# Experts with 640 slots, results scattered straight to the output, weights cast in the load

## The chip, the core and the metric

The kernel runs on one core of a Trainium2 chip. The core has five engines with a queue of instructions each: TensorE (PE, matrix multiplication; PEld is its loading of weights), VectorE (DVE), ScalarE (ACT), GpSimd (POOL) and SyncE (SP). Sixteen DMA engines move data between DRAM and the on-chip memory SBUF; a transfer is issued by an instruction on the queue of SP, ACT or POOL. The engines run apart from one another and wait on semaphores. PSUM is the memory that matmuls write to. The metric is device time in microseconds (us) of one execution.

## The reference

Attention with a bias by relative distance, then a layer of eight experts that each token is sent to by a hash of its id. There are 8 batches, 8 heads, 576 positions and 64 values a head, so 4608 tokens of 512 values; an expert has a hidden layer of 1024.

```python
scores = scale * q @ k.T + bias_table[bucket(|i - j|)]     # 8 x 8 heads, 576 x 576
attn   = softmax(scores);  x = attn @ v                     # 4608 rows of 512
e      = token_ids * 2654435761 % 8                         # one expert a token
out[i] = relu(x[i] @ w1[e[i]]) @ w2[e[i]]                   # w1 512x1024, w2 1024x512
```

The multiplier is 1 modulo 8, so the expert is the low three bits of the token id. The inputs are a fixed draw, with 584, 594, 556, 565, 570, 567, 568 and 604 tokens for experts 0 to 7.

## The kernel before

The program is written with a library that tracks which instruction reads or writes which tile or DRAM tensor, adds the waits, and orders each engine's queue with a planner of its own: it goes by the order of the program, but lets an instruction that is ready rise past others that are not. The order in a queue is therefore not that of the text. In the trace the zero fill written after batch 0 (L357) is issued at 19.84 us, and the load of the first expert's w1, written in batch 4 (L373), at 96.10 us.

**Set-up (L89 to L183).** The exponential of the bias goes over a small DRAM tensor t_ebp. From the token ids the kernel works out, for each token, its slot: 768 (CAP) times its expert plus its rank among that expert's tokens. The ids are read so that the token's position is on the partitions, one 4-byte word at a time. The ranks come from a one-hot tile by a doubling sum on DVE and a triangular matmul. The slots are ds2.

**Attention (L186 to L364).** For each batch v is loaded on SP's queue, and q and k on POOL's, which turns them from 32 to 16 bits on the way. Four head pairs follow. For each pair PE transposes q and k (L251), forms scores (L289), ACT takes the exponential (L297), DVE multiplies by the bias tile (L305), PE multiplies with v (L330), and DVE divides into x_sb (L348). The bias tiles are made in batch 0, per head, by two transfers on SP's queue (L195, t_ebr from t_ebp, and L203, the tile from t_ebr). Finished 128-row groups of x_sb are scattered by POOL into the DRAM tensor t_xperm at their slots (L364), 36 groups in all. t_xperm was filled with zeros before (L357), by SP.

**Experts (L379 to L457).** For expert e the kernel loads w1 and w2 in 32 bits on SP's queue (L414, L422), casts them on ACT (L419) and on DVE (L427), loads the expert's 768 rows (xpn, L388), transposes them on PE (L399, copied by DVE at L404), multiplies by w1 (L434; 2 halves of 384 columns, 8 blocks of the hidden layer, 4 steps each), takes ReLU on ACT (L440) and multiplies by w2 (L448; 6 groups of 128 rows, 8 steps each). DVE copies each group to a tile ok (L455, four buffers), and SP writes it to the DRAM tensor t_pout (L457). The transposes of the next expert stand between the two layers. The first expert's w1 is loaded and cast during attention (L373, L377).

**Tail (L458 to L468).** For each of 36 groups of tokens, POOL gathers the rows from t_pout at the same slots (L460), into one of twelve tiles, and SP writes the tile to the output (L468).

Of the kernel before, what the change touches and what calls it, by code (L numbers as in the profile page):

```python
# [11 lines left out]
F32 = mybir.dt.float32  # L12
F16 = mybir.dt.float16
I32 = mybir.dt.int32
AF = mybir.ActivationFunctionType
# [16 lines left out]
def kernel(  # L32
# [23 lines left out]
    CAP = 768  # L56
    NSLOT = E * CAP
    NPT = DM // P
# [13 lines left out]
    SLT_np = np.triu(np.ones((P, P), dtype=np.float32), 1)  # L72
    Z_np = np.zeros((P, DM), dtype=np.float16)
# [4 lines left out]
    Z_d = nc.inline_tensor(Z_np, "t5_zero")  # L78
# [4 lines left out]
    xperm_d = nc.dram_tensor("t5_xperm", [NSLOT, DM], F16, kind="Internal")  # L83
    pout_d = nc.dram_tensor("t5_pout", [NSLOT, DM], F32, kind="Internal")

# [5 lines left out]
    w1f0 = cst.tile([P, NPT, F], F32, name="w1f0")  # L91
    w1h0 = cst.tile([P, NPT, F], F16, name="w1h0")

    with tc.tile_pool(name="su", bufs=1, side="right") as su, tc.tile_pool(
# [18 lines left out]
        sltsb = su.tile([P, P], F32, name="sltsb")  # L113
        nc.sync.dma_start(out=sltsb[:, :], in_=SLT_d.ap())

        tid32 = moe_token_ids.bitcast(I32)
        e2i = su.tile([P, NGT], I32, name="e2i")
        with nc.allow_non_contiguous_dma("tiny index reshape"):
            nc.sync.dma_start(
                out=e2i[:, :],  # L120
                in_=bass.AP(tid32.tensor, 0, [[2, P], [2 * P, NGT]]),
            )
        ei = su.tile([P, NGT], I32, name="ei")
        nc.vector.tensor_scalar(
            out=ei[:, :], in0=e2i[:, :], scalar1=E - 1, scalar2=None,
            op0=ALU.bitwise_and,
        )
        ef = su.tile([P, NGT], F32, name="ef")
        nc.vector.tensor_copy(out=ef[:, :], in_=ei[:, :])

        oh = su.tile([P, E, NGT], F32, name="oh")
        for e in range(E):
# [4 lines left out]
        rowtot = su.tile([P, E], F32, name="rowtot")  # L137
        nc.vector.tensor_reduce(
            out=rowtot[:, :], in_=oh[:, :, :], axis=mybir.AxisListType.X,
            op=ALU.add,  # L140
        )
        partA = sup.tile([P, E], F32, name="partA", space=bass.MemoryType.PSUM)
        nc.tensor.matmul(out=partA[:, :], lhsT=sltsb[:, :], rhs=rowtot[:, :])

        pa = su.tile([P, E, NGT], F32, name="pa")
        pb = su.tile([P, E, NGT], F32, name="pb")
        nc.vector.tensor_copy(out=pa[:, :, :], in_=oh[:, :, :])
        cur, nxt = pa, pb
        sh = 1
        while sh < NGT:  # L150
            nc.vector.tensor_copy(out=nxt[:, :, :sh], in_=cur[:, :, :sh])
            nc.vector.tensor_tensor(
                out=nxt[:, :, sh:], in0=cur[:, :, sh:],
                in1=cur[:, :, : NGT - sh], op=ALU.add,
            )
            cur, nxt = nxt, cur
            sh *= 2
        exc = nxt
        nc.vector.tensor_tensor(
            out=exc[:, :, :], in0=cur[:, :, :], in1=oh[:, :, :], op=ALU.subtract  # L160
        )
        for e in range(E):
            nc.vector.tensor_scalar(  # L163
                out=exc[:, e, :], in0=exc[:, e, :],
                scalar1=partA[:, e : e + 1], scalar2=None, op0=ALU.add,
            )
        nc.vector.tensor_tensor(
            out=exc[:, :, :], in0=exc[:, :, :], in1=oh[:, :, :], op=ALU.mult
        )
        rank = su.tile([P, NGT], F32, name="rank")  # L170
        nc.vector.tensor_reduce(
            out=rank[:, :], in_=exc[:, :, :].transpose([0, 2, 1]),
            axis=mybir.AxisListType.X, op=ALU.add,
        )
        dsf = su.tile([P, NGT], F32, name="dsf")
        nc.vector.tensor_scalar(
            out=dsf[:, :], in0=ef[:, :], scalar1=float(CAP), scalar2=None,
            op0=ALU.mult,
        )
        nc.vector.tensor_tensor(  # L180
# [318 lines left out]
```

The softmax here doesn't subtract the row's maximum and nothing guards it: scores larger than these inputs give would overflow.

## Time and profile before

| | |
|---|---|
| median of 3 runs | 699.89 us (699.37 to 702.21) |
| span of the profiled execution (the page gives no other time of it) | 705.6 us |
| set-up and wait for the first bias tile | 0 to 57.4 us |
| attention | 57.4 to 440.5 us |
| last scatters and first load of rows | 440.5 to 463.6 us |
| experts | 463.6 to 643.6 us |
| tail | 643.6 to 705.6 us |
| busy: PE, DVE, ACT, POOL | 556.6, 343.5, 290.3, 139.7 us |
| DMA queues: hardware_dynamic (SP), software_dynamic (POOL) | 86.28 MB, 23.60 MB |

The page cuts the span in 40 slices of 17.6 us and gives each engine's busy share of a slice as a digit of tenths. Groups of instructions carry their line, engine, what they write and read, count, busy time and mean; after the second bar stands the idle time of the engine before them and what ended it. The chain is followed back from the last instruction to what released it, and its parts are given as start, duration and what. A timeline's line has start, duration, engine, line and instruction, and in brackets the idle time before it with its releaser. In a table of stretches the DMA share is the sum of the time of packets over 16 engines, so it can pass 1 where packets overlap. Bytes are those written: the q and k loads count at 16 bits.

### The profile page before, as it was taken

To read this page: it belongs to the slowest core of one execution; us is meant where nothing else is said; L and a number is where in the kernel's file an instruction comes from. 1 tells how busy PE (TensorE), PEld (TensorE's weight loads), DVE (VectorE), ACT (ScalarE), POOL (GpSimd) and SP (SyncE) were. 2 spreads that over 40 slices of the span, in tenths; PEclk is the share of its full clock that TensorE was granted. 3 is DMA by queue.
4 is the path that set the end of the run, shared out by engine and by line. 5 is a ranking of instruction groups with operands and counts; after the bars stand their busy time and mean duration, and the time that the engine had idled before them with its cause. 6 is when DMAs were issued, how large, how long until landed. Compare 5 with 4: busy or idle time off the path is not lost.

```text
span 705.6 us, 9655 instructions
## 1 busy us (share of the span) xinstructions
PE 556.6 (79%) x3656; PEld 287.1 (41%) x3656; DVE 343.5 (49%) x1150; ACT 290.3 (41%) x458; POOL 139.7 (20%) x156
## 2 busy tenths in 40 slices
PE   2626999999999999999999998089999999994000
PEld 0202545444444545454444544055555555552000
DVE  3305666666676766667666666024433343312000
ACT  1312365545545453645445463044466545440000
POOL 7213001412323124114110200200000000002772
PEclk9999999999999999999999999999999999998555
DMA  9999980900905819409300000197999997113998
GB/s 111 307 206 262 274 220 24 134 25 18 132 31 33 103 39 67 84 16 86 72 15 1 31 1 1 53 380 278 322 370 334 326 359 265 45 76 127 359 392 283
DMA packets 159614, 110.49 MB, mean 157 GB/s; under 512 B 120520, under 2 KB 131912, under 8 KB 159472
## 3 DMA queue, kind: packets, MB, share of 16 engines
q1 hardware_dynamic: 79952, 86.28, 39.0%
q0 software_dynamic: 79616, 23.60, 26.9%
q8 instruction: 28, 0.46, 0.3%
q14 instruction: 18, 0.15, 0.1%
HBM read 92.55 MB, written 35.54 MB: 182 GB/s over the span
## 4 chain that ended last, share of the span: by engine, by line
PE 64%; DMA 10%; ACT 9%; issue 5%; DVE 3%; POOL 3%; SPq 3%; POOLq 0%; ACTq 0%
PE px L330 22%; PE sc L289 15%; PE ops L448 11%; PE hps L434 11%; ACT attn L297 8%; DMA t_ebr<-t_ebp 3%; POOL og L460 3%; DVE attn L305 3%; PE psq L251 3%; SPq L218 2%; PE psk L251 2%; DMA t_xperm<-x_sb,ds 2%; DMA ebias<-t_ebr 1%; DMA w1f<-in_moe_w_dram 1%; PE xps L399 1%
## 5 line engine op out<-in xcount | busy, mean ns | idle before, releaser
L297 ACT ACTIVATE attn<-sc 128x576 f16<-128x576 f32 (+1 forms) x320 | 197.4, 647 | 224.6 <-PE sc L289 198.4
L330 PE MATMUL px<-vaug,attn 128*128 128x65 f16 (+3 forms) x1600 | 182.4, 243 | 20.0 <-DVE attn L305 16.8
L289 PE MATMUL sc<-qT,kT 64*128 64x512 f16 (+3 forms) x640 | 178.0, 428 | 24.6 <-ACT attn L297 24.4
L305 DVE TENSOR_TENSOR attn<-attn,ebias 128x576 f16<-128x576 f16 (+1 forms) x320 | 139.3, 452 | 90.5 <-ACT attn L297 57.6
L330 PEld LDWEIGHTS <-attn 128*128 128x128 f16 (+3 forms) x1600 | 117.4, 122 | 126.5 <-DVE attn L305 77.4
L440 ACT ACTIVATE h<-hps 128x384 f16<-128x384 f32 x128 | 62.2, 490 | 98.3 <-PE hps L434 97.5
L434 PE MATMUL hps<-xpt,w1h 128*128 128x384 f16 x512 | 86.6, 330 | 1.5 <-ACT h L440 1.5
L448 PE MATMUL ops<-w2h,h 128*128 128x512 f16 x384 | 86.6, 379 | 0.0
L364 POOL DMA_INDIRECT t_xperm<-x_sb,ds x36 | 37.6, 1044 | 243.6 <-DVE x_sb L348 178.2
L289 PEld LDWEIGHTS <-kT 64*128 64x128 f16 (+1 forms) x640 | 46.4, 116 | 79.6 <-issue 71.5
L460 POOL DMA_INDIRECT og<-t_pout,ds x36 | 34.1, 947 | 205.3 <-DMA t_pout<-ok 193.2
L348 DVE TENSOR_SCALAR x_sb<-px,rcp 128x64 f16<-128x64 f32 (+1 forms) x320 | 70.0, 274 | 1.6
L434 PEld LDWEIGHTS <-w1h 128*128 128x128 f16 x512 | 50.6, 99 | 36.3 <-issue 3.5
L455 DVE COPY ok<-ops 128x512 f32<-128x512 f32 x48 | 33.1, 691 | 59.5 <-PE ops L448 53.3
L448 PEld LDWEIGHTS <-h 128*128 128x128 f16 x384 | 37.1, 98 | 41.2
L224 POOL DMA_DIRECT2D qb<-in_q_dram x40 | 35.4, 886 | 82.7 <-PE psk L251 73.8
L404 DVE COPY xpt<-xps 128x768 f16<-128x768 f16 x32 | 17.2, 556 | 62.5 <-PE xps L399 61.6
L343 DVE RECIPROCAL rcp<-px 64x1 f32<-64x1 f32 (+1 forms) x128 | 18.7, 167 | 51.9 <-PE px L330 48.9
L251 PE MATMUL psq<-ident,qb 128*128 128x128 f16 (+1 forms) x160 | 35.6, 292 | 9.0 <-DVE pb L163 5.1
L228 POOL DMA_DIRECT2D kb<-in_k_dram x40 | 35.3, 882 | 21.9 <-DMA kb<-in_k_dram 21.8
L251 PE MATMUL psk<-ident,kb 128*128 128x128 f16 (+1 forms) x160 | 36.3, 297 | 0.0
L399 PE MATMUL xps<-ident,xpn 128*128 128x128 f16 x192 | 15.9, 230 | 22.1 <-DMA xpn<-t_xperm 22.1
(37 smaller groups left out, 182.5 us busy)
## 6 DMA issues: line engine op xcount, KB each, us to landing
w1f<-in_moe_w_dram SPq DMA_DIRECT2D x8, 2048.0 KB
w2f<-in_moe_w_dram SPq DMA_DIRECT2D x8, 2048.0 KB
t_pout<-ok SPq DMA_DIRECT2D x48, 256.0 KB
out_dram<-og SPq DMA_DIRECT2D x36, 256.0 KB
vb<-in_v_dram SPq DMA_DIRECT2D x32, 256.0 KB
xpn<-t_xperm SPq DMA_DIRECT2D x8, 768.0 KB
ebias<-t_ebr SPq DMA_DIRECT2D x8, 720.0 KB
qb<-in_q_dram POOLq DMA_DIRECT2D x32, 128.0 KB
```

What stands on the lines that cost most here:

```text
L224: nc.gpsimd.dma_start(out=qb16[:nt, t, :, :], in_=q[b, :, P * t : P * t + nt, :].transpose([1, 0, 2]),)
L251: nc.tensor.transpose(out=pst[:, P * t : P * t + nt], in_=srct[:nt, t, 2 * m : 2 * m + 2, :], identity=ident[:nt, :nt],)
L289: nc.tensor.matmul(out=scps[hh][:nt, ns:ne], lhsT=kT[64 * hh : 64 * hh + 64, P * t : P * t + nt], rhs=qT[64 * hh : 64 * hh + 64, ns:ne], s ...
L297: nc.scalar.activation(out=attn[hh][:nt, t, :], in_=scps[hh][:nt, :], func=AF.Exp, bias=0.0, scale=scale,)
L305: nc.vector.tensor_tensor(out=attn[hh][:nt, t, :], in0=attn[hh][:nt, t, :], in1=ebias[2 * m + hh][:nt, NJT - 1 - t, :], op=ALU.mult,)
L330: nc.tensor.matmul(out=px[nbase : nbase + isz, c, :], lhsT=attn[hh][:nt, t, i0c : i0c + isz], rhs=vaug[hh][:nt, t, :], start=(imm == 0), s ...
L348: nc.vector.tensor_scalar(out=x_sb[nbase : nbase + isz, gt, h * D : (h + 1) * D], in0=px[nbase : nbase + isz, c, :D], scalar1=rcp[nbase : ...
L364: nc.gpsimd.indirect_dma_start(out=xperm_d.ap()[:, :], out_offset=bass.IndirectOffsetOnAxis(ap=ds2[:, g : g + 1], axis=0), in_=x_sb[:, g, ...
L434: nc.tensor.matmul(out=hps[:, :], lhsT=w1h[:, kt, ts(ft, P)], rhs=xpt[kt][:, ts(nr, NR)], start=(kt == 0), stop=(kt == NPT - 1),)
L440: nc.scalar.activation(out=h1[:, ft, ds(nr * NR, NR)], in_=hps[:, :], func=AF.Relu, bias=0.0, scale=1.0,)
L448: nc.tensor.matmul(out=ops[:, :], lhsT=h1[:, ft, ts(kc, P)], rhs=w2h[:, ft, :], start=(ft == 0), stop=(ft == NFT - 1),)
L460: nc.gpsimd.indirect_dma_start(out=og[:, :], out_offset=None, in_=pout_d.ap()[:, :], in_offset=bass.IndirectOffsetOnAxis(ap=ds2[:, g : g + ...
```

## The change

Each expert gets 640 slots instead of 768. Tokens beyond 640 of an expert go to extra rows of t_xperm, one for each token, and are worked by a separate path at the end, inside a branch on a flag that the set-up computes (some expert has more than 640 tokens). A row of t_xperm is 514 instead of 512 values: the last two hold the token's number as a 32-bit integer, and rows without a token hold a number out of range. After the second layer POOL scatters each 128 rows straight to the output, at the numbers that came along with the rows; rows out of range are left out. t_pout and the tail are gone.

The weights are loaded on POOL's queue and turned to 16 bits by the transfer, into two tiles each for w1 and w2 that last the whole kernel; those of experts 0 and 1 are written in batches 3 and 5 of attention, those of e+2 after the layer of e that frees the tile. Loads of rows are written two experts ahead, three buffers. In the first layer one activation covers both halves (320 columns each). The set-up reads the ids in rows of 128 and transposes them on PE, takes the ranks from two matmuls and a scan, and the fill of t_xperm is issued from ACT's queue, from an SBUF tile.

```diff
-    CAP = 768
+    CAP = 640
     NSLOT = E * CAP
+    NROW = NSLOT + B * S
+    BIG = 1 << 20
...
+    XW = DM + 2
+    xperm_d = nc.dram_tensor("t5_xperm", [NROW, XW], F16, kind="Internal")
...
+    w1t = [cst.tile([P, NPT, F], F16, name=f"w1t{i}") for i in range(2)]
+    w2t = [cst.tile([P, NFT, DM], F16, name=f"w2t{i}") for i in range(2)]
+    def load_w1(e):
+        nc.gpsimd.dma_start(
+            out=w1t[e % 2][:, :, :],
+            in_=moe_w1[e].rearrange("(kt p) f -> p kt f", p=P),
+        )
+    def load_w2(e):
+        nc.gpsimd.dma_start(
+            out=w2t[e % 2][:, :, :],
+            in_=moe_w2[e].rearrange("(ft p) d -> p ft d", p=P),
+        )
...
-                in_=bass.AP(tid32.tensor, 0, [[2, P], [2 * P, NGT]]),
+        er = su.tile([NGT, 2 * P], I32, name="er")
+        nc.sync.dma_start(
+            out=er[:, :],
+            in_=bass.AP(tid32.tensor, 0, [[2 * P, NGT], [1, 2 * P]]),
+        )
...
+        zx = su.tile([P, XW], F16, name="zx")
+        nc.vector.memset(zx[:, :DM], 0.0)
+        nc.vector.memset(zx[:, DM:XW].bitcast(I32), BIG)
+        nc.scalar.dma_start(
+            out=xperm_d.ap()[:NSLOT, :].rearrange("(p r) d -> p r d", p=P),
+            in_=zx[:, :].unsqueeze(1).to_broadcast([P, NSLOT // P, XW]),
+        )
...
-            if b == 0:
-                nc.sync.dma_start(
-                    out=xperm_d.ap().rearrange("(a b) d -> a (b d)", b=64),
...
-            if b == 4:
-                nc.sync.dma_start(
-                    out=w1f0[:, :, :],
-                    in_=moe_w1[0].rearrange("(kt p) f -> p kt f", p=P),
-                )
-                nc.scalar.copy(out=w1h0[:, :, :], in_=w1f0[:, :, :])
+            if b == 3:
+                load_w1(0)
+                load_w2(0)
+            if b == 5:
+                load_w1(1)
+                load_w2(1)
...
+            xpn = mo.tile([P, NSC, XW], F16, name="xpn", bufs=3)
...
+        xn = {0: x_load(0), 1: x_load(1)}
+        xt = {0: x_transpose(xn[0])}
         for e in range(E):
...
+            if e + 2 < E:
+                xn[e + 2] = x_load(e + 2)
+            w1h, w2h = w1t[e % 2], w2t[e % 2]
...
+            for ft in range(NFT):
+                hps = mop.tile([P, NRC, 512], F32, name="hps", bufs=2,
+                               space=bass.MemoryType.PSUM)
+                for nr in range(NRC):
...
+                nc.scalar.activation(
+                    out=h1[:, ft, :].rearrange("p (r n) -> p r n", r=NRC),
+                    in_=hps[:, :, :NR], func=AF.Relu, bias=0.0, scale=1.0,
+                )
+            if e + 2 < E:
+                load_w1(e + 2)
+            if e + 1 < E:
+                xt[e + 1] = x_transpose(xn[e + 1])
+            for kc in range(NSC):
+                ops = mop.tile([P, DM], F32, name="ops", bufs=2,
+                               space=bass.MemoryType.PSUM)
...
                 ok = mo.tile([P, DM], F32, name="ok", bufs=4)
                 nc.vector.tensor_copy(out=ok[:, :], in_=ops[:, :])
-                nc.sync.dma_start(out=pout_d.ap()[ts(kg, P), :], in_=ok[:, :])
-        for g in range(NGT):
...
+                nc.gpsimd.indirect_dma_start(
+                    out=out[:, :],
+                    out_offset=bass.IndirectOffsetOnAxis(
+                        ap=xn[e][:, kc, DM:XW].bitcast(I32), axis=0
+                    ),
+                    in_=ok[:, :],
+                    in_offset=None,
+                    bounds_check=N - 1,
+                    oob_is_err=False,
+                )
+            if e + 2 < E:
+                load_w2(e + 2)
+
+    over = nc.values_load(flag[:1, :1], min_val=0, max_val=1)
+    with tc.If(over > 0):
...
```

What is left out after the branch is the path for tokens beyond 640: for each expert it loads both weights again and runs a loop of 36 turns, each with a gather, both layers for 128 rows and a scatter.

## The prediction

> **What bounds the kernel now.** I read the page's slices first, then the stretches with the engines' busy times, the chain that ended last, and the engines' own timelines. The four stretches that matter, with the columns us, then busy time (instructions) of PE, PEld, DVE, ACT, POOL, then PE clock, DMA share, GB/s:
>
> ```profile
> PE   2626999999999999999999998089999999994000
> DMA  9999980900905819409300000197999997113998
> ...
> 440.40:463.60 23.20, 2.05 (x19) 1.92 (x20) 1.79 (x6) 0.00 (x0) 4.80 (x5) 1.00 0.36 115
> 463.60:705.60 242.00, 178.47 (x1072) 98.11 (x1070) 66.77 (x86) 87.00 (x135) 34.08 (x36) 0.88 0.77 278
> 643.60:705.60 62.00, 0.00 (x1) 0.00 (x0) 0.69 (x1) 0.00 (x0) 34.08 (x36) 0.54 0.87 312
> ```
>
> Attention occupies 57 to 440 us with PE full; a gap follows; the experts run to 643.6; then PE is idle for 62.0 us while rows are gathered and written. So everything after the first expert matmul is 242.0 us, and this is where the change acts. In the expert stage PE has no pauses worth naming: one expert, from its first matmul to the next one's, is 578.56 - 556.41 = 22.15 us.
>
> ```profile
> 556.41 10.40 PE hps L434 x64
> 566.81 0.67 PE xps L399 x12
> ...
> 568.84 9.71 PE ops L448 x45
> 578.56 10.40 PE hps L434 x64
> ```
>
> The gap and the start are DMA. Five scatters stand one behind another at the end of attention; each waits for the one before to have landed (same columns as the timeline: start, us, engine, line, then in brackets the idle time and what ended it):
>
> ```profile
> 443.62 0.96 POOL L364 DMA_INDIRECT t_xperm<-x_sb,ds  x1 [2.20 <-DMA t_xperm<-x_sb,ds]
> 446.78 0.96 POOL L364 DMA_INDIRECT t_xperm<-x_sb,ds  x1 [2.19 <-DMA t_xperm<-x_sb,ds]
> ...
> 648.52 0.97 POOL L460 DMA_INDIRECT og<-t_pout,ds  x1 [0.30 <-issue]
> 649.79 0.94 POOL L460 DMA_INDIRECT og<-t_pout,ds  x1 [0.30 <-issue]
> ```
>
> The reader should see the two paces: scatters into one DRAM tensor come every 3.15 us, gathers into separate tiles every 1.25 us. The difference is a wait of a write for the write before it, not the cost of an indirect transfer.
>
> In the start, this stretch of the chain leads to the first multiplication with the bias at 57 to 60 us (start, us, what):
>
> ```profile
> 18.73 6.73 DMA t_ebp<-ebsb
> 26.01 23.56 DMA t_ebr<-t_ebp
> 49.63 10.16 DMA ebias<-t_ebr
> ```
>
> 0.9 MB of t_ebr takes 23.56 us because the 6.3 MB zero fill was issued at 19.84 us on the same SP queue, just ahead.
>
> **The change, part by part.**
>
> *Slots, 768 to 640.* Of 22.15 us, 64 matmuls of the first layer take 10.40 (384 columns, 162.5 ns each); at 320 columns 135.4 ns, so 8.67. The second layer has 40 matmuls instead of 48: 10.36 to 8.63. Transposes 20 instead of 24: 1.39 to 1.16. PE's time of an expert becomes 18.45 us. ReLU on 640 columns: the 576-column activation takes 647 ns and the 384-column one 490, so about 0.70 us against the 1.08 us in which PE fills it; hidden.
>
> *Weights cast in the DMA.* ACT's cast (3.60 us) and DVE's (2.28) go; both lie beside PE in the expert stage. The one of w1h0 at 118.28 us isn't hidden: that head pair took 132.68 - 118.11 = 14.57 instead of 12.2 us; I take -2.4. The loads move to POOL's queue, which the page calls software_dynamic, and of which there is one. How long is a 2 MB load there? Before shows no such load, so I bound it. From below: the uncast loads of the same size move 393 GB/s in 466 to 474 us, 5.3 us. From above: the q and k loads are cast, in runs of 256 B, and their 128 KB (after the cast) come every 0.87 us, which is 301 GB/s of fp32; POOL's issue sets that pace, so a 2 MB load needs at most 7.0 us unless long runs are slower than short ones. I take T = 6.
>
> *Scatter of the results.* Removed: 48 writes to t_pout and the tail's 36 gathers and 36 output writes, 62.0 us on the path. Added: 40 scatters on POOL, all into the one tensor out. By the rows at 443 us I expect each to wait for the one before: s = 3.15 us with 1 KB rows is the low end; these rows have 2 KB, so the part that is neither issue nor pause (3.15 - 0.96 - 0.71 = 1.5 us) at most doubles: 4.6 is the high end. The bytes alone at 393 GB/s add 0.33, so I take s = 3.5.
>
> Now what is queued behind what. POOL's order in the stage is w1(e+2), five scatters, w2(e+2), w1(e+3), five scatters. One queue drains in order (t_ebr behind the fill is the row for that), so the first scatter of an expert lands only after two loads have. Let t0 be the first expert matmul. First layer done at 8.7; w1(2) issued (0.9), 0.4 to start; scatter 0 lands at 11.6 + T (1.6 for its own landing); the fifth starts 0.7 + 3s later, at T + 12.3 + 3s = 28.8. From the fifth scatter of one expert to that of the next: two issues and a start 2.0, two loads 2T, landing 1.9, pause 0.7, 3s: 2T + 4.6 + 3s; the first issue overlaps by 0.3, so 2T + 4.3 + 3s = 26.8 us. That is longer than PE's 18.45: POOL's queue becomes the bound. Five such intervals; one with one load (T + 4.3 + 3s); one with none (5s); the last landing (s). Sum: 12T + 38.1 + 27s = 72 + 38.1 + 94.5 = 204.6 us. The ends are 187 (5.3; 3.15) and 246 (7.0; 4.6).
>
> PE isn't a second bound in that loop: with four ok tiles it runs a whole expert ahead of the scatters, so the load of w1(e+3) finds its buffer free when POOL comes to it. Were it not so, up to 8.7 us an expert would be added.
>
> A rule speaks against this part. POOL's issue of a scatter takes 0.96 us at the end of attention, where DVE is idle, and up to 1.30 in the middle. The Trainium skill (SBUF — State Buffer, "Who interferes with whom") says that copies in DVE's two-port modes shut GpSimd out of a shared port, and advises issuing from ACT or SP. If it held here at the 1.30 end, 27 x 0.34 = 9 us would be added; DVE's copies in this stage read PSUM, so I leave the sum.
>
> *Overflow path.* The drawn token ids give 556 to 604 tokens an expert, all below 640, so the branch isn't taken. The flag's load and the jump over the branch have no row; the chain's last piece, 1.16 us on POOL's sequencer, is the nearest. Bounds 0 and 10 (five engines with a few such pieces); I take 5, nearer to neither, since every engine has to read the flag.
>
> So from the first expert matmul: 209.6 against 242.0, -32.4.
>
> *Gap.* xpn shrinks from 768 to 640 rows of 1028 B instead of 1 KB: 4.79 to about 4.3; -0.5. Five scatters stand as before.
>
> *Start.* Three things move. The token ids came as 4608 runs of 4 B ahead of the v loads on SP, landing at 11.7 us; now 36 rows. The fill goes to ACT's queue, 5.26 MB, early, so t_ebr no longer stands behind it: at the 10.16 us of the three times larger ebias load it could take 15 us less. Against it: the scheduler lets independent loads rise (w1f0, written in batch 4, was issued at 96.1 us; the fill, written after batch 0, at 19.84), and POOL stands idle from 24.8 to 36.7, so the four weight loads, 8.4 MB instead of 2.1, may fall into this stretch: at 393 GB/s 16 us more DMA beside the bias loads. The fill also occupies ACT's queue ahead of the exponential that feeds t_ebp. Bounds -15 and +12; I take -5. The Trainium skill (DMA: Bandwidth & Descriptors, "Queues, rings and completion order") has each engine take turns between queues, packet by packet; by that the bias loads would get half of the rate, and -5 would be about 0.
>
> The set-up's DVE operations are each under 0.7 us and end before 26 us, beside the wait for bias; nothing.
>
> Sum: -32.4 - 2.4 - 0.5 - 5 = -40.3. The profiled execution has a span of 705.6 us (the page gives no other time for it), 5.7 over the median of the runs, 699.9; I carry the difference: 665.3 by the span, 660 by the median.
>
> **The rivals.**
>
> *PE stays the bound.* If scatters into out don't wait for one another, or the loads don't hold them up, eight experts take 8 x 18.45 = 148, plus last copy, scatter and branch, some 9: 157 against 242, with the rest -93: 607; with a pace of five scatters plus two issues (19.3 us) 615. For it: the gathers' 1.25 us. Against: all 36 scatters before have the wait.
>
> *The cast loads are slow (slower than before).* Each us of T costs 12. With 2.4, 0.5 and 5 gained elsewhere the balance turns where 12T + 137.6 = 250, T = 9.4 us, 224 GB/s. At T = 12 the time is 732. For it: no long cast in the trace; against: 301 GB/s on much shorter runs.
>
> *The start gets dearer.* If weights and fill delay the bias loads by 12 instead of helping by 5, 677. For it: DMA digits of 9 through the first 88 us.
>
> **How the numbers follow.** Forecast (POOL's queue the bound) 0.62, 660; its own range 630 to 695 from the ends of T, s and the start taken one at a time. PE the bound 0.14, 611. Dear start 0.10, 677. Slow casts 0.14, above 700. The range 606 to 704 leaves out the slow case and a sliver. About 0.5% (3.5 us) is what a measurement can tell from no change. Faster: 0.60 + 0.14 + 0.09 = 0.83; within: 0.04; slower: 0.13.
>
> **What would show it.** In the profile after: POOL the releaser, with scatter waits on "DMA out"; a period of some 27 us from expert to expert; PE's idle time in the stage ended by weight or ok waits; first-layer matmuls of 320 columns near 135 ns; no gather tail; the first bias multiplication before 57 us. I am wrong if scatters come under 2 us apart (then 611), if w1 or w2 takes over 9 us to land, or if the first scatter of x, at 99.0 us before, starts later.

## The result and the profile after

The changed kernel takes 722.05 us (median of 5 runs, 720.98 to 726.58) where the kernel before takes 699.89 (median of 5, 698.62 to 702.21): 1.0325 times as long, interval 1.0293 to 1.0357. It is slower, and the time lies above the range of the prediction (606 to 704). The profiled executions differ by 724.7 - 705.6 = 19.1 us.

The slices of the changed kernel, and its table of stretches cut at the same events as before (first bias multiplication, last scatters of x, first expert matmul, end; columns as in the prediction):

```profile
PE   2016069999999999999999999834997769569670
DMA  9999997409149093091391000003477656766511
...
0.00:94.60 94.60, 19.03 (x76) 6.33 (x76) 10.54 (x49) 9.81 (x14) 26.62 (x35) 1.00 1.37 177
94.60:477.60 383.00, 357.08 (x2493) 180.68 (x2493) 262.47 (x1004) 190.21 (x308) 76.90 (x84) 1.00 0.47 65
477.60:501.40 23.80, 1.68 (x15) 1.54 (x16) 1.57 (x6) 0.00 (x0) 4.79 (x5) 1.00 0.33 105
501.40:724.70 223.30, 160.31 (x980) 92.27 (x977) 41.76 (x71) 45.05 (x64) 49.89 (x52) 0.86 0.54 115
```

Read against the table of before, the four stretches were 57.4, 383.0, 23.2 and 242.0 us. The tail is gone (no slices of PE 0 at the end), and the experts with all behind them take 18.7 us less. Attention and the gap stand still within 1 us. The start takes 37 us more. That is the whole result: -18.7 in the stage that was forecast to give -32.4, +37 where -5 was forecast.

**The start.** SP's queue in the changed kernel, from its timeline (start, duration, queue, line, instruction), then DVE's first bias multiplication:

```profile
3.65 57.90 SPq L267 DMA_DIRECT2D vb<-in_v_dram  x10
61.68 3.68 SPq L130 DMA_DIRECT2D t_ebp<-ebsb  x1
76.61 1.84 SPq L244 DMA_DIRECT2D t_ebr<-t_ebp  x3
83.25 4.55 SPq L252 DMA_DIRECT2D ebias<-t_ebr  x3
```

```profile
94.56 1.92 DVE L354 TENSOR_TENSOR attn<-attn,ebias 128x576 f16<-128x576 f16 x5 [27.29 <-DMA ebias<-t_ebr]
```

The same in the kernel before:

```profile
3.07 15.55 SPq L218 DMA_DIRECT2D vb<-in_v_dram  x5
18.73 1.06 SPq L111 DMA_DIRECT2D t_ebp<-ebsb  x1
19.84 0.56 SPq L357 DMA_DIRECT2D t_xperm<-t_zero  x1
...
57.44 1.93 DVE L305 TENSOR_TENSOR attn<-attn,ebias 128x576 f16<-128x576 f16 x5 [23.50 <-DMA ebias<-t_ebr]
```

From the table t_ebp all bias tiles are made. Ahead of it now stand ten loads of v instead of five, and they take 57.9 us in all instead of 15.6. It goes out 43 us later (61.68 against 18.73). From there to the first multiplication it is 32.9 us instead of 38.7, so the gain that the prediction saw behind t_ebp is there, 5.8 us, and is dwarfed by what happened ahead of it. The lines of DMA queues and issues on the changed kernel's page show what the v loads ran beside, and the waits of SP's queue what they waited for (who, for what, us in total, times, longest):

```profile
q10 hardware_dynamic: 5136, 5.26, 4.3%
...
t_xperm<-zx ACTq DMA_DIRECT2D x1, 5140.0 KB, 47.8
...
SPq L267 <- DMA t_xperm<-zx: 23.2, 1, 23.2
```

The fill, now on a queue of its own, went out at 1.64 us and landed 47.8 us later, in 5136 packets of about 1 KB. Four loads of v went out by 26.3 us; the fifth waited 23.2 us, until the fill had landed at 49.4, and the last six took from 49.45 to 61.56. The wait is the program's, not one for data: in the trace the transfers of SP and ACT take eight semaphores in turn (108 to 115) to signal that they have landed, and each first waits for the transfer that had its semaphore before; the fill had 111, and so has the fifth load.

**The experts.** POOL's timeline over one expert of the changed kernel; in brackets the idle time before each instruction and what ended it:

```profile
565.20 0.98 POOL L489 DMA_INDIRECT out_dram<-ok,xpn  x1 [7.64 <-DMA out_dram<-ok,xpn]
566.33 0.81 POOL L102 DMA_DIRECT2D w1t<-in_moe_w_dram  x1 [0.16 <-issue]
568.58 1.00 POOL L489 DMA_INDIRECT out_dram<-ok,xpn  x1 [1.45 <-DMA out_dram<-ok,xpn]
577.49 0.97 POOL L489 DMA_INDIRECT out_dram<-ok,xpn  x1 [7.91 <-DMA out_dram<-ok,xpn]
581.91 0.97 POOL L489 DMA_INDIRECT out_dram<-ok,xpn  x1 [3.45 <-DMA out_dram<-ok,xpn]
582.88 0.97 POOL L108 DMA_DIRECT2D w2t<-in_moe_w_dram  x1
585.41 1.00 POOL L489 DMA_INDIRECT out_dram<-ok,xpn  x1 [1.56 <-issue]
593.57 0.99 POOL L489 DMA_INDIRECT out_dram<-ok,xpn  x1 [7.16 <-DMA out_dram<-ok,xpn]
```

Each scatter waits for the one before to land. Quiet ones follow every 3.5 us (581.91 to 585.41); one that is under way beside a weight load holds the next back for 8 to 9 us (568.58 to 577.49, 585.41 to 593.57). Five gaps, two of them long, make 28.4 us an expert. The page's groups tell who pays:

```profile
L488 DVE COPY ok<-ops 128x512 f32<-128x512 f32 x40 | 27.7, 691 | 138.2 <-DMA out_dram<-ok,xpn 121.0
L489 POOL DMA_INDIRECT out_dram<-ok,xpn x40 | 39.2, 981 | 155.0 <-DMA out_dram<-ok,xpn 120.3
```

DVE's copy out of PSUM finds no free ok tile for 121 us, because a tile is free only when its scatter has landed, and PE's second layer stops behind DVE (37.6 us on the page).

### The profile page after: what moved, and what is told of

Same layout as the page of the kernel before. It is cut to its first block, busy times and chain, and to the rows that moved or that the text cites. A ratio compares the mean times of both kernels' runs of the same rounds, so it can differ in the third digit from the quotient of the medians.

```text
span 724.7 us, 9277 instructions
## 1 busy us (share of the span) xinstructions
PE 538.1 (74%) x3561; PEld 280.8 (39%) x3561; DVE 316.3 (44%) x1126; ACT 245.1 (34%) x386; POOL 158.2 (22%) x176
## 3 DMA queue, kind: packets, MB, share of 16 engines
q10 hardware_dynamic: 5136, 5.26, 4.3%
## 5 line engine op out<-in xcount | busy, mean ns | idle before, releaser
L481 PE MATMUL ops<-w2t,h 128*128 128x512 f16 x320 | 82.3, 409 | 37.7 <-DVE ok L488 37.6
L469 ACT ACTIVATE h<-hps 128x640 f16<-128x640 f32 x64 | 45.1, 704 | 175.9 <-PE hps L463 175.8
L488 DVE COPY ok<-ops 128x512 f32<-128x512 f32 x40 | 27.7, 691 | 138.2 <-DMA out_dram<-ok,xpn 121.0
L463 PE MATMUL hps<-xpt,w1t 128*128 128x320 f16 x512 | 74.1, 306 | 0.0
L489 POOL DMA_INDIRECT out_dram<-ok,xpn x40 | 39.2, 981 | 155.0 <-DMA out_dram<-ok,xpn 120.3
L481 PEld LDWEIGHTS <-h 128*128 128x128 f16 x320 | 32.2, 103 | 77.6 <-issue 48.8
L463 PEld LDWEIGHTS <-w1t 128*128 128x128 f16 x512 | 51.4, 101 | 23.6 <-issue 2.5
L273 POOL DMA_DIRECT2D qb<-in_q_dram x40 | 35.2, 879 | 99.2 <-PE psk L300 68.6
L277 POOL DMA_DIRECT2D kb<-in_k_dram x40 | 35.2, 880 | 34.9 <-DMA kb<-in_k_dram 21.8
L300 PEld LDWEIGHTS <-qb 128*128 128x128 f16 (+1 forms) x160 | 19.8, 130 | 45.9 <-issue 26.6
L448 DVE COPY xpt<-xps 128x640 f16<-128x640 f16 x32 | 15.1, 489 | 46.0 <-PE xps L444 45.0
## 6 DMA issues: line engine op xcount, KB each, us to landing
ebias<-t_ebr SPq DMA_DIRECT2D x8, 720.0 KB, 10.5
t_xperm<-zx ACTq DMA_DIRECT2D x1, 5140.0 KB, 47.8
qb<-in_q_dram POOLq DMA_DIRECT2D x32, 128.0 KB, 5.3
kb<-in_k_dram POOLq DMA_DIRECT2D x32, 128.0 KB, 5.1
```

The source lines that it names most:

```text
L273: nc.gpsimd.dma_start(out=qb16[:nt, t, :, :], in_=q[b, :, P * t : P * t + nt, :].transpose([1, 0, 2]),)
L300: nc.tensor.transpose(out=pst[:, P * t : P * t + nt], in_=srct[:nt, t, 2 * m : 2 * m + 2, :], identity=ident[:nt, :nt],)
L463: nc.tensor.matmul(out=hps[:, nr, :NR], lhsT=w1h[:, kt, ts(ft, P)], rhs=xt[e][:, kt, ts(nr, NR)], start=(kt == 0), stop=(kt == NPT - 1),)
L469: nc.scalar.activation(out=h1[:, ft, :].rearrange("p (r n) -> p r n", r=NRC), in_=hps[:, :, :NR], func=AF.Relu, bias=0.0, scale=1.0,)
L481: nc.tensor.matmul(out=ops[:, :], lhsT=h1[:, ft, ts(kc, P)], rhs=w2h[:, ft, :], start=(ft == 0), stop=(ft == NFT - 1),)
L489: nc.gpsimd.indirect_dma_start(out=out[:, :], out_offset=bass.IndirectOffsetOnAxis(ap=xn[e][:, kc, DM:XW].bitcast(I32), axis=0), in_=ok[:, :],
```

## The experiments

All are the changed kernel with edits. Ratios are to the kernel before on the same chip, with their intervals; on the chips of the experiments the kernel before took 705 to 706 us. Marks for the start are the first bias multiplication, the first scatter of x, and the first expert matmul; the stage is what follows that.

### Is the pace of the experts set by POOL's one queue?

The theory on record was that a queue drains in order, so that a scatter lands only after the load issued ahead of it. The rival: a scatter is slow beside any load in flight, and the chain of waits passes this on. First, the weights of experts 2 to 7 leave POOL's queue (w_sp):

```diff
-                load_w1(e + 2)
+                w1f = mo.tile([P, NPT, F], F32, name="w1f", tag="wf", bufs=2)
+                nc.sync.dma_start(out=w1f[:, :, :], in_=moe_w1[e + 2]...)
+                nc.scalar.copy(out=w1t[e % 2][:, :, :], in_=w1f[:, :, :])
```

(and likewise w2, cast on DVE).

> The changed kernel with the weights of experts 2 to 7 loaded in 32 bits on SP's queue and cast on ACT (w1) and DVE (w2), as before the change; those of experts 0 and 1 and the scatters to the output stay. Theory of the shared queue (loads and scatters add up on POOL's queue: 5 x 3.48 + 2 x 5.3 = 28 us an expert): POOL's part falls to 17.4 us, PE's 18.45 becomes the bound, the stage from the first expert matmul falls from 223 to about 162, and the time by 60, to about 662. Rival, the chain of scatters alone is the bound and the loads ride beside it: a period of 27 us or more an expert stays and the time falls by less than 10 us. Rival, the casts on ACT and DVE or the DMA rate take over: 22 us an expert, to about 690.

Measured: 1.0228 (1.0206 to 1.0249), stage 223.5 us against 223.3. POOL's timeline, with no load in its queue; SP issued w1 at 538.68 and w2 at 549.73:

```profile
538.85 0.97 POOL L494 DMA_INDIRECT out_dram<-ok,xpn  x1 [2.37 <-DMA out_dram<-ok,xpn]
547.46 3.08 POOL L494 DMA_INDIRECT out_dram<-ok,xpn  x1 [7.63 <-DMA out_dram<-ok,xpn]
557.80 0.97 POOL L494 DMA_INDIRECT out_dram<-ok,xpn  x1 [7.26 <-DMA out_dram<-ok,xpn]
561.30 0.97 POOL L494 DMA_INDIRECT out_dram<-ok,xpn  x1 [2.53 <-DMA out_dram<-ok,xpn]
```

The gaps are much the same, 8.6 and 10.3 us beside the two loads (2.1 of the 10.3 are the longer issue at 547.46) and 3.5 otherwise. The shared queue is not the cause. This is what the Trainium skill (DMA: Bandwidth & Descriptors, "Issuing engines are not separate DMA queues") says: transfers issued by different engines run on the same 16 DMA engines and interleave. The prediction had used the queue's order from t_ebr behind the fill, and taken it for the reason here too.

Then the waits go. Each token has one slot, so the 40 scatters write different rows; they are declared as writes to 40 disjoint views of the output (no_waw):

```diff
+        oview = dram_disjoint_views(out, E * NSC)
...
-                    out=out[:, :],
+                    out=oview[e * NSC + kc][:, :],
```

> The changed kernel with one edit: the 40 scatters to the output are declared as writes to 40 disjoint views of it (each token's number occurs once, so their rows are disjoint), so a scatter no longer waits for the one before; weights stay on POOL's queue. Theory of the chain of waits (scatters one at a time, and each that meets a 2 MB load in flight takes as long as what is left of the load): without the waits PE's 18.45 us an expert is the bound, the stage from the first expert matmul to the end falls from 223 to about 160 us, the time by about 60 us against the changed kernel. Rival, loads and scatters fill POOL's queue or the DMA engines with real work: about 28 us an expert stays and the time falls by less than 10.

And on the other side, the loads go and the waits stay (no_load): experts 2 to 7 compute with the weights of 0 and 1, so twelve 2 MB loads are left out:

```diff
-            if e + 2 < E:
-                load_w1(e + 2)
...
-            if e + 2 < E:
-                load_w2(e + 2)
```

> The changed kernel without the weight loads of experts 2 to 7: the tiles of experts 0 and 1 are used again, so the rows of those six experts are multiplied by other weights and the output is not the reference's; all the rest is done. Theory that a load in flight is what lengthens a scatter: every scatter comes at 3.5 us, five are 17.4 us, PE's 18.45 is the bound, and the stage falls from 223 to about 165 us. Rival, the scatters' own chain is slow also without loads: a period of 25 us or more an expert stays, above 210 us.

Measured: no_waw 0.9244 (0.9207 to 0.9280), stage 159.0 us; no_load 0.9451 (0.9403 to 0.9498), stage 172.4 us. The loads alone, beside scatters that don't wait, cost nothing that can be seen, as PE's own pace below shows; so the waits alone cost 172.4 - 159.0 = 13 us, and both together 64. The stage of no_load is longer than expected (165): beside a load of rows the next scatter comes after 4.5 to 5.4 us, and a few others late in the stage, whose cause was not looked for, come after 4.6 to 5.6. PE's timeline of no_waw, from one expert's first layer to the next one's:

```profile
529.39 8.86 PE L465 MATMUL hps<-xpt,w1t 128*128 128x320 f16 x64
...
539.88 8.15 PE L483 MATMUL ops<-w2t,h 128*128 128x512 f16 x37
547.86 8.86 PE L465 MATMUL hps<-xpt,w1t 128*128 128x320 f16 x64
```

547.86 - 529.39 = 18.47 us, PE's own time. POOL's timeline of the same kernel shows the scatters behind DVE's copy, not behind one another:

```profile
543.85 0.99 POOL L491 DMA_INDIRECT out_dram<-ok,xpn  x1 [0.72 <-DVE ok L490]
545.58 0.97 POOL L491 DMA_INDIRECT out_dram<-ok,xpn  x1 [0.74 <-DVE ok L490]
547.30 0.97 POOL L491 DMA_INDIRECT out_dram<-ok,xpn  x1 [0.75 <-DVE ok L490]
```

So the chain of waits is the cause, and a load in flight, on POOL's queue or on SP's, is its multiplier. The start in these two kernels is the changed kernel's (first scatter of x at 126.9 and 128.0 us), and no_waw is faster than the kernel before all the same.

### What makes the start dear?

Three suspects stood in the traces: ten loads of v ahead of t_ebp, the fill in short runs on its own queue, and 8.4 MB of weights loaded early (issued at 57.8 to 64.0 us, around t_ebp, not at 25 to 37 as one expectation below has it). One run for each. v_wait holds the loads of v for batch 1 until the first bias tile is there, so that five stand ahead of t_ebp as before:

```diff
+            if b == 1:
+                nc.vector.tensor_copy(out=vb[:1, :, 0, :1], in_=ebias[0][:1, :, :1])
```

> The changed kernel with one edit: the v loads of batch 1 wait for the first bias tile, so that only five v loads stand ahead of t_ebp on SP's queue, as before the change. Everything else, the fill of t_xperm from ACT's queue included, stays. Queue-order theory: t_ebp is issued at about 3.65 + 5 x 5.8 = 33 us instead of 61.7, the first bias multiplication comes at about 66 instead of 94.6, and the time falls by 29 us, from 722 to about 693. Rival, the fill: its 5140 runs of 1028 B occupy the DMA engines until 49 us whatever stands on SP's queue, t_ebp, t_ebr and the bias tile are slowed themselves, and the first multiplication comes at 78 or later; the time falls by 16 us at most, to 706. Rival, the early weight loads: no change, 722.

fill_old puts the fill back: from a DRAM constant, in runs of 66 KB, on SP's queue, written after batch 0.

```diff
-        nc.scalar.dma_start(
-            out=xperm_d.ap()[:NSLOT, :].rearrange("(p r) d -> p r d", p=P),
-            in_=zx[:, :].unsqueeze(1).to_broadcast([P, NSLOT // P, XW]))
...
+            if b == 0:
+                nc.sync.dma_start(
+                    out=xperm_d.ap()[:NSLOT, :].rearrange("(a b) d -> a (b d)", b=64),
+                    in_=bass.AP(Z_d.ap().tensor, 0, [[0, NSLOT // 64], [1, 64 * XW]]))
```

> The changed kernel with the fill of t_xperm undone: written after batch 0, from a DRAM constant in long runs, on SP's queue, as before. With it the planner also puts only five v loads ahead of t_ebp again. Queue-order theory and fill theory both: the first bias multiplication comes at 57 us or a little earlier and the time falls by 37 to 42 us, to about 682. Early-weights theory: the four weight loads, now at 25 to 37 us, lie beside t_ebr and the bias tiles; the first multiplication comes at 70 or later and the fall is 25 us or less, to 697 or more. How much this falls below the run in which only the order of v loads is changed is the price of the fill itself.

w_late makes the weights of experts 0 and 1 wait for the rows that batches 3 and 5 finish, by a copy of one such element into the weight tile ahead of each load:

```diff
+                gl = ((b + 1) * S) // P - 1
+                for wt in (w1t[i], w2t[i]):
+                    nc.vector.tensor_copy(
+                        out=wt[:1, 0, :1], in_=x_sb[:1, gl, DM - 1:DM])
                 load_w1(i)
                 load_w2(i)
```

> The changed kernel with one edit: the weight loads of experts 0 and 1 wait for rows that batches 3 and 5 finish, so none lies in the start. Early-weights theory: from the issue of t_ebp to the first multiplication 25 us or less instead of 32.9, and less waiting for bias in batch 0; the time falls by 8 to 15 us, to 707 to 714. Queue-order and fill theories: t_ebp is issued at about 61.7 us as before, and the time falls by at most 4 us, to 718 or more.

The start of w_sp is the changed kernel's, on the same chip, and serves as the mark:

| kernel | ratio, interval | v loads ahead of t_ebp | t_ebp issued | first bias mult. | first scatter of x | first expert matmul | stage |
|---|---|---|---|---|---|---|---|
| w_sp (start unchanged) | 1.0228 (1.0206 to 1.0249) | 10 | 58.5 | 87.7 | 132.0 | 495.5 | 223.5 |
| v_wait | 1.0079 (1.0048 to 1.0111) | 5 | 48.2 | 70.9 | 122.7 | 486.5 | 224.1 |
| w_late | 1.0042 (1.0017 to 1.0067) | 10 | 57.3 | 76.6 | 119.5 | 483.2 | 223.4 |
| fill_old | 0.9798 (0.9773 to 0.9823) | 5 | 13.0 | 50.7 | 106.6 | 467.5 | 219.7 |

Each helps, the fill most: with it alone undone the change is 1.5 to 2% faster than the kernel before (the second run of it stands below).

In v_wait t_ebp goes out at 48.2 us, not at the 33 that a pace of 5.8 us a load gives: the fifth load waits for the fill here too, 22.2 us, until 46.2. So the fill's landing holds t_ebp back first, and the five further loads add some 10 us to it. In w_late, where t_ebp is as late as in w_sp, the first multiplication follows it by 19.3 us instead of 29.3: early weights cost about 10 us behind t_ebp. SP's queue in fill_old:

```profile
3.55 9.33 SPq L263 DMA_DIRECT2D vb<-in_v_dram  x5
13.00 1.11 SPq L133 DMA_DIRECT2D t_ebp<-ebsb  x1
14.16 0.61 SPq L402 DMA_DIRECT2D t_xperm<-t_zero  x1
```

Undoing the fill also undoes the ten v loads, since the planner places five ahead of t_ebp again, and none of them waits for the fill, which now goes out behind them; they issue in 1.9 us each. With fill_old t_ebp goes out at 13.0 us, 5.7 before the old kernel's, and the first bias multiplication comes at 50.7, 6.7 before. That the token ids no longer stand ahead of v as 4608 runs of 4 B is the likely reason; it was not tried alone. The gains overlap and don't add. Fill and weights together (old_wlate, the edits of fill_old and w_late in one):

> Both edits of the start together: the fill from DRAM on SP's queue after batch 0, and the weights of experts 0 and 1 loaded only after rows of batches 3 and 5. If the fill and the early weight loads are the two causes and add up, the first scatter of x comes at 90 to 96 us (99.0 in the kernel before, 106.6 with the fill alone undone), and the time is 10 to 16 us below the run with the fill alone undone, 0.955 to 0.965 of the kernel before. If the early loads only matter beside the short-run fill: within 4 us of that run.

Measured: 0.9722 (0.9674 to 0.9769), first scatter at 97.7 us, first expert matmul at 461.3. Against fill_old that is 0.8% more (1.2% against its second run), less than the expectation had. Beside the short-run fill the same edit gave 1.9% (w_sp to w_late), so a part of the early weights' harm came with the fill.

### The fill: its runs or its place?

fill_old changed run length, source, queue and moment at once. Three more kernels fill in the other corners. old_short has the fill in the old place, in runs of 1028 B (one row):

```diff
+                    out=xperm_d.ap()[:NSLOT, :].rearrange("(r p) d -> p r d", p=P),
+                    in_=bass.AP(Z_d.ap().tensor, 0, [[XW, P], [0, NSLOT // P], [1, XW]])
```

> As the run with the fill on SP's queue from DRAM, but the fill cut into 5120 runs of 1028 B instead of 80 blocks of 64 rows; bytes, queue and place in the order stay. Theory of short runs (what makes the fill dear is its many small pieces, wherever they are issued): the fill takes 40 us or more instead of under 20, t_ebr behind it lands 20 us later, and the time is 15 to 25 us above that run. Rival, the fill is dear because it is issued from ACT at the very start, ahead of all and on a queue of its own: the same time as that run within 4 us.

long_wlate has it in the new place from an SBUF tile of 40 rows a partition, in runs of 41 KB, with the late weights of w_late:

```diff
-        zx = su.tile([P, XW], F16, name="zx")
+        zx = su.tile([P, NSLOT // P, XW], F16, name="zx")
...
-            in_=zx[:, :].unsqueeze(1).to_broadcast([P, NSLOT // P, XW]),
+            in_=zx[:, :, :].rearrange("p r d -> p (r d)"),
```

> The changed kernel with the fill still early, on ACT's queue and from SBUF, but in runs of 41 KB instead of 1028 B (40 rows next to one another in the tile), and the weights of experts 0 and 1 held back. If the short runs are what makes the fill dear: fill landed in under 25 us instead of 44 to 48, first scatter of x near 100 to 108 us, first expert matmul near 465 to 470, ratio 0.975 to 0.985. If its place on ACT's queue or the early issue is what costs, the first scatter stays at 119 us and the ratio at 1.00, as with the weights held back alone.

Its fill landed in 18.7 us instead of 43.8, but its start did not follow (1.0075, 1.0052 to 1.0098; first scatter at 119.6 us). Its timeline shows why. (In the kernel before and in the changed one POOL's first load of q goes out at 1.27 us.)

```profile
34.68 0.20 DVE L235 COPY x_sb<-tok 128x36 int32<-128x36 int32 x1 [16.17 <-DMA t_xperm<-zx]
35.23 1.06 POOL L273 DMA_DIRECT2D qb<-in_q_dram  x1 [34.79 <-DMA t_ebr<-t_ebp]
```

The first loads of q and v go out at 35.2 and 34.6 us, and the fill, issued at 15.86, landed at 34.6. DVE's first write to x_sb, at 3.11 us in the changed kernel, waits for the fill here, though it has no data from it. The set-up's memory is used again by attention's tiles; that these lay over the large tile and waited for the fill to have read it fits the times, and in act_long, which has no such tile, the first loads go out at 1.27 and 4.04 us. (The q load waits for several transfers, and the profile puts its wait down to t_ebr.) The run tells of run length and the fill's time, not of its place. act_long leaves that tile out: new place, long runs from the DRAM constant of fill_old.

```diff
-            in_=zx[:, :].unsqueeze(1).to_broadcast([P, NSLOT // P, XW]),
+            in_=bass.AP(Z_d.ap().tensor, 0, [[0, NSLOT // 64], [1, 64 * XW]]),
```

> The changed kernel with its fill still the first transfer on ACT's queue, at the place of the changed kernel, but from a DRAM constant in runs of 64 rows, 66 KB each, as the kernel before had it on SP's; no large tile in SBUF stands in the way, as it did with the fill of 41 KB runs. If the run length is what costs, whatever the queue and the moment: fill landed in under 22 us, first bias multiplication by 55 us, first scatter of x at 100 to 108, ratio 0.975 to 0.99, like the fill in the old place. If the queue and the early issue cost as much as the run length: first scatter near 118 to 122 us, ratio 1.00, like the short runs in the old place. If the source, not the run length, made the old fill cheap, the fill lands in over 40 us.

> The fill as before (same long runs, SP's queue, after batch 0) once more, as the mark for the other run of this group. Both theories expect the ratio measured, 0.98, and the first scatter of x at 105 to 108 us.

Measured, with the first scatter of x behind each ratio; the changed kernel is shown as it was measured on two chips, the second beside long_wlate (after_again):

> The changed kernel once more, beside the three others of this group, so that they are read against it on the same chip. Both theories (the loss lies in the start; the loss lies in the expert stage) expect the ratio already measured, 1.03, first scatter of x between 127 and 137 us, expert stage 223 us.

| | runs of 66 KB | runs of 1028 B |
|---|---|---|
| SP's queue, after batch 0 | fill_old 0.9798, 106.6 us; again 0.9846 (0.9816 to 0.9875), 108.1 us | old_short 1.0020 (0.9999 to 1.0041), 118.7 us |
| first on ACT's queue | act_long 0.9989 (0.9971 to 1.0006), 116.2 us | after 1.0325, 137.4 us; after_again 1.0223 (1.0193 to 1.0252), 131.6 us |

Short runs cost 1.7 to 2.2% in the old place and 2.3 to 3.4% in the new one; the new place costs 1.4 to 1.9% with long runs and 2.0 to 3.1% with short ones. Both matter, about alike. In one cell, first on ACT's queue in 1028 B runs, the fill comes from SBUF and in the other three from DRAM; the long runs landed alike from both (18.7 us in long_wlate, 21.0 in act_long), so the source is not what made it long. The lines of DMA queues on the page give the size of the first (time of the packets as a share of 16 engines over the span); act_long:

```profile
q10 hardware_dynamic: 176, 5.26, 2.3%
```

2.3% of 16 x 701.7 us is 258 us of engine time for 5.26 MB; in the changed kernel 4.3% of 16 x 724.7 is 499 us, 97 ns a packet, and in the six other kernels with the same fill 395 to 466. The place works through SP's queue: in act_long too ten v loads come ahead of t_ebp, and the second of them waits until the fill has landed, at 21.7 us:

```profile
4.04 37.99 SPq L269 DMA_DIRECT2D vb<-in_v_dram  x10
43.27 0.33 SPq L133 DMA_DIRECT2D t_ebp<-ebsb  x1
...
SPq L269 <- DMA t_xperm<-t_zero: 17.3, 1, 17.3
```

In every kernel with the fill first on ACT's queue a load of v waits for the fill, for 15.6 to 23.2 us, and in none with it on SP's. This joins run length and place: a fill in short runs lands later, and the wait passes that on to t_ebp. No run took the wait alone away.

Every kernel with the fill first on ACT's queue has the ten, but for v_wait, where they are held back, and long_wlate; every one with it on SP's has five. Why the planner orders so was not tested.

### All three repaired

old_wlate_nowaw has the edits of fill_old, w_late and no_waw together.

> The changed kernel with three edits: the fill as before (long runs, SP's queue, after batch 0), the weights of experts 0 and 1 held back to batches 3 and 5, and the 40 scatters of results without waits for one another. If the losses in the start and in the chain of scatters are separate and add up: first expert matmul at 461 us as with the first two edits alone, stage of 159 us as with the third alone, span 620, ratio 0.885. If the fill and the chain share a cause (the stage's loads are only fast because the start is slow, or the other way round), the stage comes out above 165 us or the first expert matmul above 470.

old_wlate_nowaw_sp has the edit of w_sp besides.

> As old_wlate_nowaw, but the weights of experts 2 to 7 are loaded in 32 bits on SP's queue and cast on ACT (w1, 3.6 us) and DVE (w2, 2.3 us), as the kernel before did. If the cast in the transfer is worth something by itself once no scatter waits, this one is slower, by the time that ACT's cast keeps the ReLU back: up to 3.6 us for each of six experts, 22 us, ratio 0.91. If the casts hide beside TensorE's 18.45 us, as they did in the kernel before, the two ratios agree within 0.005. POOL's issue of a scatter should again be 3 us beside DVE's cast, six scatters, and cost nothing, since nothing waits for them.

Measured: 0.8851 (0.8832 to 0.8869) and 0.8809 (0.8791 to 0.8826). The first has its first expert matmul at 461.0 us and a stage of 160.6: the repairs add up. The slices and the stretches of attention and experts in old_wlate_nowaw:

```profile
PE   3037999999999999999999999999149999999992
...
50.20:432.80 382.60, 355.37 (x2472) 178.87 (x2471) 260.00 (x997) 191.27 (x310) 85.44 (x95) 1.00 0.57 79
461.00:621.60 160.60, 149.10 (x980) 90.33 (x977) 41.79 (x71) 45.06 (x64) 49.64 (x52) 0.98 0.73 160
```

PE is full from 50 us to the end but for the gap. Casting in the transfer is worth nothing by itself here: with the casts back on ACT and DVE, beside PE, the kernel is 0.4% faster, not the 2.5% slower that one theory had; its period after the first expert is 18.47 us but for one of 18.69, and the difference lies after the last scatter's issue (7.4 us to the end instead of 10.5), which was not followed further. The six scatter issues that meet DVE's cast take 2.77 us each there, and nothing waits for them. Both beat the kernel before and the changed one by over 11%.

## Why the prediction was wrong

Signed by term, in the profiled executions:

| term | forecast | measured | from |
|---|---|---|---|
| start | -5 (bounds -15, +12) | +38.4 | first scatter of x, 99.0 to 137.4 us |
| w1h0's cast | -2.4 | -1.3 | first to last batch's scatter, 341.5 to 340.2 us |
| gap | -0.5 | +0.7 | 23.1 to 23.8 us |
| experts | -32.4 | -18.7 | 242.0 to 223.3 us |
| sum | -40.3 | +19.1 | spans |

**The step that failed is the start.** The prediction followed t_ebr and ebias and asked what would stand ahead of them in their queue. That half came out right: 5.8 us less from t_ebp to the first multiplication. Its two parts were about of the size worked out for them: without the early weights (w_late) this piece is 19.3 us instead of 38.7, and with them 29.3 (w_sp) to 32.9, where the prediction had up to 15 us less by the fill and 16 us more by the weights' bytes. What was not followed is t_ebp itself. It stands behind loads of v on SP, whose number, pace and waits were left as they were. They did not stay: the order of SP's queue changed to ten v loads, and the fifth waited 23.2 us for the fill, which landed after 47.8 us in its 1028 B runs, where runs of 66 KB from the same queue landed after 21.0 (act_long). So t_ebp went out 43 us later. The text noted that the fill would be early and that independent loads rise; it applied this to the weights and not to v, the loads next to t_ebp in the very queue. And it gave no price to the fill's new access pattern, of which no row of before showed the like.

**The rival "the start gets dearer"** was the right one at a third of its price: +12 for 677, where the start alone gave +38. It had the bias loads delayed by weights and fill; most of the delay came earlier, at t_ebp. Added to the measured stage this decides the sign.

**The experts' term had the right pace by a wrong reason.** The forecast's parts were 28.8 us to the fifth scatter, five intervals of 26.8, 38.3 for the two last experts and 8.5 for the last landing and the branch. Measured: 35.9; 143.1 in all, 28.6 each; 35.3; 8.9. The first and third differ because the planner put w2(2) ahead of the fifth scatter; together they cost 4.1. The intervals cost 9.1, as a scatter beside a load takes 8.5 us (mean of the twelve) and a quiet one 3.6 (mean of the other 27; the loads of rows go out beside those of w1). s = 3.5 was right. T, as the time by which a load lengthens a scatter's gap, came out at 5 instead of 6; a whole load lands 9.6 to 9.9 us after its issue (medians), which is above the 9.4 of the "slow casts" rival and the 9 named as a sign of being wrong, but that is not what the chain pays. That PE would run a whole expert ahead of the scatters failed: with four ok tiles it stops behind them. This hardly lengthens the chain: DVE's copy to ok ends two of the 39 waits between scatters.

The reason given, that POOL's one queue drains loads and scatters in order, fell to w_sp. **The rival "PE stays the bound"** had its price right: 157 us for the stage, against 159.0 once the waits were gone, and 18.45 us an expert against 18.47. The slots' terms (8.67 and 8.63 us) fit there: they add up to that pace. The waits, which that rival needed gone, were there, as forecast.

The note on the shared port came out as taken: POOL's scatter issue averages 0.98 us in the stage, where DVE's copies read PSUM. The branch's price was never isolated; 8.9 us from the last scatter's issue to the end bounds it together with a landing.

Two of the prediction's numbers don't come out as worked, and neither decides anything. Taken one at a time, as it says, the ends of T, s and the start give 650 to 690, not 630 to 695. And an ebias load is 2.4 times one of t_ebr (720 against 303.8 KB), not three.

## What to carry to other kernels

When a change moves a bulk transfer to another queue, ask what it will run beside, not only what it no longer stands in front of; follow the chain that sets the start back to its very first link, look in the queue's waits for one that the data don't ask for, and price an access pattern that the trace doesn't show from both sides, far apart. Scattered writes to disjoint rows of one tensor are worth declaring as disjoint: a write that waits for the write before it pays its whole landing time, and that time is two to three times as long while a 2 MB load is in flight, on either queue tried here. Casting weights in the transfer bought nothing where the casts already lay beside PE.

## What the runs showed of the hardware

- Run length of a plain write: 5.26 MB to DRAM in 1028 B runs, first on ACT's queue, took 395 to 499 us of DMA engine time in seven kernels and landed in 41 to 48 us where the page has the landing; in 41 or 66 KB runs 193 and 258 us, and 18.7 and 21.0 us (from SBUF and from DRAM, same queue).
- A scatter of 128 rows of 2 KB lands so that the next one goes 3.5 us later; beside a 2 MB load the gap is 8 to 10 us, on the same queue (8.2 to 9.8 in eleven of twelve) and on another (8.6 and 10.3 above, with 2.1 us of longer issue in the latter). Without waits the scatters go out every 1.73 us beside the same loads: the wait, not the rate, was the cost.
- POOL's issue of a scatter took 0.97 us, and 3.08 when it met DVE's cast of w2 from SBUF to SBUF (w_sp; the cast runs from 547.41 for 2.28 us, the issue from 547.46). The Trainium skill (SBUF — State Buffer, "Who interferes with whom") names casts among DVE's operations that can shut GpSimd out of their shared port; this case agrees. By moving that cast into the transfer the change avoids it, which is worth nothing as long as POOL is not the bound.
- The load that casts 2 MB from 32 to 16 bits can run at least at PE's pace: two in 18.47 us an expert (no_waw), with nothing waiting for them.
